# Attention scores of both heads in one full-height product, from batch 3 on

## The chip, the cores and the metric

The kernel runs on one core of a Trainium2 chip. Its time is the device time of one launch in microseconds (us), the median of three runs. One further run was made under the hardware profiler; "the profile" and "the trace" are of that run. TensorE is called PE in it, VectorE DVE, ScalarE ACT, GpSimd POOL and SyncE SP. Line numbers (L266 and so on) are those of the kernel before.

## What is computed

Eight batches of eight heads, 576 positions, head dimension 64. Each head has causal attention with a sparse mask: the first four heads of a batch see the last 32 positions, the last four see the positions of the same remainder modulo 32. The 4608 rows of 512 values that come out go through a two-layer projection with a leaky activation in between.

```python
scores = scale * np.matmul(q, k.transpose(0, 1, 3, 2))
mask_local = (rel >= 0) & (rel < stride)                       # stride = 32
mask_strided = (rel >= 0) & (pos[None, :] % stride == pos[:, None] % stride)
...                                                            # local for h < 4, strided for h >= 4
attn = np.exp(scores - max); attn = attn / (sum + 1e-09)
x = (attn @ v).transpose(0, 2, 1, 3).reshape(B * S, H * D)
h = x @ w_in                                                   # 512 -> 2048
g = np.maximum(h, 0.0) + alpha * np.minimum(h, 0.0)
out = g @ w_out                                                # 2048 -> 512
```

## The kernel before

All products are in 16-bit floats with 32-bit sums. A **unit** is half a batch, four local or four strided heads; a unit has two **pairs** of heads, numbered g from 0 to 31. The two heads of a pair lie one above the other in the partitions: head 0 in rows 0 to 63, head 1 in rows 64 to 127.

The attention is cut into small pieces, each a Python function that issues its instructions for all engines:

- `transpose_piece(u, "q")` and `(u, "k")`: eight PE transposes (L209) of a unit's queries or keys into a PSUM tile tp, and copies from there to SBUF: from batch 2 on one copy on DVE for queries (to qT, L156) and one on ACT for keys (to kT, L154). Each covers 128 rows and 1024 elements. After the keys, `tails` does the last 64 positions of both: two or four more transposes (L232, L237) and small copies, queries on DVE and keys on ACT.
- `score_piece(P, i)`: a pair has two. For every block of queries (96 of a local pair, 72 of a strided one) and for each head there is a product (L266) of the head's 64 rows of kT with its 64 rows of qT. Head 0 writes one PSUM bank of the tile sp, head 1 another. A local piece has three blocks, six products; a strided one four blocks, eight products. ACT takes the exponential of both banks at once into an SBUF tile et (L290), and from batch 2 on POOL multiplies it with a mask of zeros and ones (L300).
- `pv_piece(P, a)`: et is the stationary operand, the values with a column of ones the moving one (L313). DVE takes reciprocals of the sums (L320) and scales (L322).
- `x_piece(P)`: PE transposes (L330) and a copy to xT (L334 on ACT for strided pairs, L338 on DVE for local ones).

The projections are cut into pieces too. `lin1_piece(n, m)` makes 128 hidden features of 512 rows: four products of 512 columns (L483), or eight where the rows wrap round in xT; then ACT makes `neg` (L493), and the DVE instruction L496, which makes gT and frees the PSUM tile hps, is put on a list `late` and issued after the next attention piece. `lin2_piece(n, i)` makes four products (L528) of the 16 that add into one PSUM tile ops; after the sixteenth ACT copies it out (L533).

The order on every engine is the program's, and it is written out by hand: the function `tile_strided_..._kernel` alternates projection pieces with attention pieces (`attn_step`). Batches 0 and 1 run partly by themselves at the start. Batch 2 lies among the second-layer pieces of row block 0 and the first half of block 1; batch 3 lies where two pieces of the first layer come on each one of the second; batches 4 to 7 lie among alternating lin2 and lin1 pieces of row blocks 2 to 5. The last projections have no attention left beside them.

PSUM buffers: three of the tag "ps" (tp, the tails' tt, pv and xp take turns), two of "hps", one "ops" and one "sp" of two banks. POOL's queue also issues most loads and casts queries and keys to 16 bits; SP's queue issues later local loads and the stores.

Of the kernel before, what the change touches and what calls it, by code (L numbers as in the profile page):

```python
# [9 lines left out]
F32 = mybir.dt.float32  # L10
F16 = mybir.dt.float16
ALU = mybir.AluOpType
AF = mybir.ActivationFunctionType
# [18 lines left out]
def kernel(  # L32
# [10 lines left out]
    nc = tc.nc  # L43
    keep = tc.keep_in_program_order

    B, H, S, D = q.shape
    NT = B * S
    NCH = NT // 512
    SCALE = 1.0 / float(np.sqrt(D))
# [4 lines left out]
    cpool = ctx.enter_context(tc.tile_pool(name="const", bufs=1))  # L54
# [10 lines left out]
    pbpool = ctx.enter_context(tc.tile_pool(name="pb", bufs=1, space=bass.MemoryType.PSUM))  # L65
# [5 lines left out]
            name=nc.get_next_instruction_name(), act_func_set_id=6, ins=[], outs=[]  # L71
# [4 lines left out]
    alpha_r = cpool.tile([16, 128], F32)  # L76
    oma = cpool.tile([128, 16], F32)
    madd = cpool.tile([128, 360], F16)
    ident = consts[:, 0:128]
    mfirst, mother, mstr = consts[:, 128:416], consts[:, 224:320], consts[0:72, 416:488]  # L80

# [3 lines left out]

    NE = 6
    qTs = [cpool.tile([128, 2, S], F16, name=f"qT{i}") for i in range(2)]
    kTs = [cpool.tile([128, 2, 672], F16, name=f"kT{i}") for i in range(2)]
    vls = [cpool.tile([128, 24, 65], F16, name=f"vl{i}") for i in range(2)]
    vss = [cpool.tile([128, 4, 8, 65], F16, name=f"vs{i}") for i in range(2)]  # L90
    ets = [cpool.tile([128, 640], F16, name=f"et{i}") for i in range(NE)]


    loaded = {}
# [57 lines left out]
    def cast_copy(eng, o, i):  # L152
        if eng == "act":
            keep(nc.scalar.copy(o, i))  # L154
        elif eng == "dve":
            keep(nc.vector.tensor_copy(o, i))  # L156
        else:
            keep(nc.gpsimd.tensor_copy(o, i))
# [18 lines left out]
    ectr = {"i": 0}  # L177
    wide = {"on": True}
    NEARLY = 2

    def make_pair(g):
        P = Pair()
        P.g, P.b, P.hp = g, g // 4, g % 4
        P.strided = P.hp >= 2
        P.pr = P.hp % 2
        P.n, P.w = (8, 72) if P.strided else (6, 96)
        u = g // 2
        P.qT, P.kT = qTs[u % 2][:, g % 2], kTs[u % 2][:, g % 2]
        P.sgroups = ([0, 1, 2, 3], [4, 5, 6, 7]) if P.strided else ([0, 1, 2], [3, 4, 5])
        P.pgroups = ([0, 1, 2], [3, 4, 5], [6, 7]) if P.strided else P.sgroups  # L190
        P.et = {}
        P.x16 = None
        return P

    def transpose_piece(u, nm):

        b, strided = u // 2, u % 2 == 1
        early = b < NEARLY
        src = cast16[(b, strided, nm)]
        dst = qTs[u % 2] if nm == "q" else kTs[u % 2][:, :, 32:608]
        tp = pspool.tile([128, 8, 64, 2], F16, tag="ps", name="tp")
        for j in range(8):
            blk = (src[:, j % 2, 128 * (j // 2) : 128 * (j // 2) + 128] if strided
                   else src[:, j].rearrange("p f d -> p (f d)"))
            keep(nc.tensor.transpose(tp[:, j].rearrange("r p e -> r (p e)"), blk, ident))  # L209
        if strided:  # L210
            main = tp.rearrange("r j p e -> r e j p")
            o = dst.rearrange("r e (j p) -> r e j p", j=8)[:, :, :, 0:64]
        else:
            main = tp.rearrange("r t p e -> r e p t")
            o = dst[:, :, 0:512].rearrange("r e (p t) -> r e p t", t=8)
        if early:
            for e in range(2):
                eng = "dve" if (nm == "q") == (e == 0) else "act"
                if nm == "k" and e == 1:
                    tails(b, u, strided)  # L220
                cast_copy(eng, o[:, e : e + 1], main[:, e : e + 1])
            return
        cast_copy("dve" if nm == "q" else "act", o, main)
        if nm == "k":
            tails(b, u, strided)

    def tails(b, u, strided):
        tl = cast16[(b, strided, "tail")]
        tt = pspool.tile([128, 1024], F16, tag="ps", name="tt")
        if strided:  # L230
            for h in range(4):
                keep(nc.tensor.transpose(  # L232
                    tt[:, 64 * h : 64 * h + 64], tl[0:64, 128 * h : 128 * h + 128],
                    ident[0:64, 0:64]))
        else:
            for e in range(2):
                keep(nc.tensor.transpose(  # L237
                    tt[:, 128 * e : 128 * e + 128], tl[:, 128 * e : 128 * e + 128], ident))
        for i, (o, eng) in enumerate(((qTs[u % 2], "dve"), (kTs[u % 2][:, :, 32:608], "act"))):
            if strided:  # L240
                tv = tt[:, 0:256].rearrange("r (e f i p t) -> r i e t f p", e=2, f=2, i=2, p=8)
                ov = o.rearrange("r e (t f p) -> r e t f p", t=4, f=2)
                for e in range(2):
                    cast_copy(eng, ov[:, e, :, :, 64:72], tv[:, i, e])
            else:
                tv = tt[:, 0:256].rearrange("r (e i p) -> r i e p", e=2, i=2)
                cast_copy(eng, o[:, :, 512:576], tv[:, i])

    def score_piece(P, i):

        et = ets[ectr["i"] % NE]
        if wide["on"] and ectr["i"] % 2:
            sps = [phpool.tile([128, 512], F32, tag="hps", name="sph") for _ in range(2)]
        else:
            sp = pbpool.tile([128, 2, 512], F32, tag="sp", name="sp")
            sps = [sp[:, y] for y in range(2)]
        ectr["i"] += 1
        w, grp = P.w, P.sgroups[i]
        n = w * len(grp)
        r = 72 if P.strided else 128  # L260
        early = P.b < NEARLY
        for x, t in enumerate(grp):
            k0 = 32 + 72 * t if P.strided else 96 * t
            for y in range(2):
                hf = slice(64 * y, 64 * y + 64)
                keep(nc.tensor.matmul(  # L266
                    sps[y][:, w * x : w * x + w], P.kT[hf, k0 : k0 + 128],
                    P.qT[hf, w * t : w * t + w], start=(x == 0),
                    stop=(x == len(grp) - 1 and not early), skip_group_check=True))

                key = (2 * (t // 2) + y, t % 2) if P.strided else (t, y)
                P.et[key] = (et, n * y + w * x)
        first = not P.strided and i == 0
        if early:

            if first:
                m = madd[:, 0:288]
            else:
                m = madd[0:72, 288:360] if P.strided else madd[:, 96:192]
                m = m.unsqueeze(1).to_broadcast([r, n // w, w])  # L280
            for y in range(2):
                keep(nc.tensor.matmul(
                    sps[y][:, 0:n], ident[0:r, :], m, start=False, stop=True, skip_group_check=True))
        ev = et[0:r, 0 : 2 * n]
        if wide["on"] and ectr["i"] % 2 == 0:
            for y in range(2):
                keep(nc.scalar.activation(
                    ev[:, n * y : n * y + n], sps[y][0:r, 0:n], AF.Exp, scale=SCALE))
        else:
            keep(nc.scalar.activation(  # L290
                ev.rearrange("r (y c) -> r y c", y=2), sp[0:r, :, 0:n], AF.Exp, scale=SCALE))
        if early:
            return
        if first:
            ev = ev.rearrange("r (y c) -> r y c", y=2)
            m = mfirst.unsqueeze(1).to_broadcast([r, 2, n])
        else:
            ev = ev.rearrange("r (c f) -> r c f", f=w)
            m = (mstr if P.strided else mother).unsqueeze(1).to_broadcast([r, 2 * n // w, w])
        keep(nc.gpsimd.tensor_tensor(ev, ev, m, op=ALU.mult))  # L300
# [38 lines left out]

    npair = 4 * B  # L340
    pairs = [make_pair(g) for g in range(npair)]
    pieces = []

# [3 lines left out]
    def T(u, nm):  # L347
        return lambda: transpose_piece(u, nm)

    def Sc(g, i):  # L350
        return lambda: score_piece(pairs[g], i)
# [40 lines left out]
    for g in range(7, npair + 2):  # L392
        a, p, t, x = g, g - 1, g + 1, g - 2
# [23 lines left out]
        todo = [(g // 4, pr) for pr in range(2)] if g % 4 == 0 and 8 <= g < npair else []  # L417

        if g % 4 == 1 and 9 <= g and g // 4 + 1 < B:
            todo = [(g // 4 + 1, nm) for nm in "qk"]  # L420
# [149 lines left out]
        keep(nc.vector.memset(kTs[i][:, :, 0:32], 0.0))  # L570
        keep(nc.vector.memset(kTs[i][:, :, 608:672], 0.0))
    for t in ets:
        keep(nc.vector.memset(t[:, 576:640], 0.0))
    keep(nc.gpsimd.memset(vls[0][0:32, 0:1, 0:64], 0.0))
    keep(nc.gpsimd.memset(vls[0][:, :, 64:65], 1.0))
    keep(nc.gpsimd.memset(vss[0][:, :, :, 64:65], 1.0))
# [37 lines left out]
            attn_step(0)  # L614

    wide["on"] = False

    for c in range(4):
        load_w(c, True)
# [83 lines left out]
```

## Time and profile before

| | |
|---|---|
| median of 3 runs | 354.89 us (353.97 to 355.74) |
| the profiled execution | 355.82 us |
| its span, first to last instruction | 354.1 us |
| mean granted TensorE clock | 0.978 |
| score products on PE (L266) | 448, from 12.6 to 261.9 us |
| query copies of 128x1024 on DVE (L156) | 12, mean 1216 ns |
| gT on DVE (L496) | 144, mean 743 ns |
| exponentials of two banks on ACT (L290) | 58, about 650 ns |
| masks on POOL (L300) | 48, mean 1281 ns |

A matmul's duration in the trace reaches from its start to the end of its own result, so neighbours overlap; the pace of PE is read from the starts. A line of the timeline merges neighbours of one kind: its duration reaches to the end of the last.

### The profile page before, as it was taken

To read this page: it belongs to the slowest core of one execution; us is meant where nothing else is said; L and a number is where in the kernel's file an instruction comes from. 1 tells how busy PE (TensorE), PEld (TensorE's weight loads), DVE (VectorE), ACT (ScalarE), POOL (GpSimd) and SP (SyncE) were. 2 spreads that over 40 slices of the span, in tenths; PEclk is the share of its full clock that TensorE was granted. 3 is DMA by queue.
4 is the path that set the end of the run, shared out by engine and by line. 5 is a ranking of instruction groups with operands and counts; after the bars stand their busy time and mean duration, and the time that the engine had idled before them with its cause. 6 is when DMAs were issued, how large, how long until landed. Compare 5 with 4: busy or idle time off the path is not lost.

```text
span 354.1 us, 6755 instructions
## 1 busy us (share of the span) xinstructions
PE 337.4 (95%) x2733; PEld 176.7 (50%) x2733; DVE 196.9 (56%) x389; ACT 178.6 (50%) x315; POOL 145.6 (41%) x163
## 2 busy tenths in 40 slices
PE   6999979999898998999999999999999999999995
PEld 2454545445444554454566674545455444444443
DVE  2367784785444777566656665666565444444400
ACT  2554863674344574556565655565555444444411
POOL 7935425439985674557355532451240000000000
PEclk9899995999999999999999999999999999999999
DMA  8999999933945772562656120000000100100021
GB/s 174 203 204 229 209 268 133 200 44 63 145 88 182 85 171 33 98 63 44 177 98 65 39 57 31 31 31 31 30 31 30 62 30 30 62 30 30 31 89 59
DMA packets 46010, 32.84 MB, mean 93 GB/s; under 512 B 27276, under 2 KB 37884, under 8 KB 45980
## 3 DMA queue, kind: packets, MB, share of 16 engines
q0 software_dynamic: 37456, 17.01, 44.8%
q1 hardware_dynamic: 8524, 15.41, 12.3%
q8 instruction: 21, 0.34, 0.4%
q14 instruction: 9, 0.07, 0.1%
HBM read 36.83 MB, written 9.44 MB: 131 GB/s over the span
## 4 chain that ended last, share of the span: by engine, by line
PE 85%; DVE 4%; POOL 4%; ACT 4%; DMA 2%; issue 1%; ACTq 0%; POOLq 0%
PE hps L483 35%; PE ops L528 32%; PE tp L209 4%; PE pv L313 3%; PE sp L266 3%; PE xp L330 2%; DMA qs<-in_q_dram 2%; DVE x L322 2%; PE wps L550 2%; POOL et L300 2%; PE ops L519 1%; DVE gT L496 1%; ACT kT L154 1%; ACT neg L493 1%; ACT osb L533 1%
## 5 line engine op out<-in xcount | busy, mean ns | idle before, releaser
L496 DVE SCALAR_TENSOR_TENSOR gT<-neg,oma,hps 128x512 f16<-128x512 f32 x144 | 106.9, 743 | 75.2 <-ACT neg L493 72.8
L483 PE MATMUL hps<-xT,win 128*128 128x512 f16 (+1 forms) x640 | 146.1, 360 | 0.1
L528 PE MATMUL ops<-wout,gT 128*128 128x512 f16 x560 | 141.9, 379 | 1.9 <-ACT osb L533 1.4
L493 ACT ACTIVATE neg<-hps 128x512 f32<-128x512 f32 x144 | 86.2, 599 | 94.2 <-PE hps L483 93.2
L300 POOL TENSOR_TENSOR et<-et,consts 128x576 f16<-128x576 f16 (+1 forms) x48 | 61.4, 1281 | 80.4 <-ACT et L290 80.2
L483 PEld LDWEIGHTS <-win 128*128 128x128 f16 x640 | 58.3, 98 | 52.5 <-issue 2.6
L528 PEld LDWEIGHTS <-gT 128*128 128x128 f16 x560 | 49.7, 98 | 50.7 <-issue 2.5
L290 ACT ACTIVATE et<-sp 72x576 f16<-72x576 f32 (+1 forms) x58 | 37.6, 649 | 21.1 <-PE sp L266 13.7
L322 DVE TENSOR_TENSOR x<-pv,rc 72x384 f16<-72x384 f32 (+2 forms) x80 | 42.1, 527 | 2.7
L320 DVE RECIPROCAL rc<-pv 72x6 f32<-72x6 f32 (+2 forms) x80 | 14.9, 186 | 42.9 <-PE pv L313 42.5
L533 ACT COPY osb<-ops 128x512 f32<-128x512 f32 x35 | 20.5, 587 | 27.9 <-PE ops L528 27.9
L313 PEld LDWEIGHTS <-et 72*128 72x128 f16 (+1 forms) x448 | 23.4, 99 | 17.9 <-issue 4.2
L266 PEld LDWEIGHTS <-kT 64*128 64x128 f16 x448 | 11.1, 96 | 25.8 <-issue 18.3
L156 DVE COPY qT<-tp 128x1024 f16<-128x1024 f16 (+1 forms) x16 | 17.4, 1084 | 6.8 <-PE tp L209 6.8
L154 ACT COPY kT<-tp 128x1024 f16<-128x1024 f16 (+1 forms) x16 | 14.5, 908 | 10.4 <-PE tp L209 10.4
L266 PE MATMUL sp<-qT,kT 64*128 64x72 f16 (+1 forms) x408 | 17.7, 202 | 1.6 <-ACT kT L154 1.0
L313 PE MATMUL pv<-vs,et 72*128 72x65 f16 x256 | 15.7, 193 | 2.5 <-ACT qT L154 1.3
L550 PE MATMUL wps<-wrm 128*128 128x512 f16 x44 | 16.3, 445 | 1.2 <-DVE wrm L562 1.2
L330 PEld LDWEIGHTS <-x 72*128 72x128 f16 (+1 forms) x224 | 12.6, 102 | 7.8 <-DVE x L322 2.4
L330 PE MATMUL xp<-consts,x 72*128 72x72 f16 (+1 forms) x224 | 14.9, 208 | 1.0 <-DVE x L322 0.8
L334 ACT COPY xT<-xp 128x576 f16<-128x576 f16 x16 | 10.2, 640 | 6.0 <-PE xp L330 5.9
L313 PE MATMUL pv<-vl,et 128*128 128x65 f16 x192 | 12.0, 200 | 1.3 <-DVE vl L156 1.1
(66 smaller groups left out, 195.4 us busy)
## 6 DMA issues: line engine op xcount, KB each, us to landing
out_dram<-osb SPq DMA_DIRECT2D x35, 256.0 KB, 2.0
ql<-in_q_dram SPq DMA_DIRECT2D x5, 512.0 KB, 4.8
kl<-in_k_dram SPq DMA_DIRECT2D x5, 512.0 KB, 6.9
vl<-in_v_dram POOLq DMA_DIRECT2D x8, 288.0 KB, 7.4
qs<-in_q_dram POOLq DMA_DIRECT2D x8, 256.0 KB, 5.5
ks<-in_k_dram POOLq DMA_DIRECT2D x8, 256.0 KB, 6.4
win<-in_moe_w_in_dram POOLq DMA_DIRECT2D x4, 512.0 KB, 11.5
wout<-in_moe_w_out_dram POOLq DMA_DIRECT2D x4, 512.0 KB, 17.9
```

What stands on the lines that cost most here:

```text
L266: keep(nc.tensor.matmul(sps[y][:, w * x : w * x + w], P.kT[hf, k0 : k0 + 128], P.qT[hf, w * t : w * t + w], start=(x == 0), stop=(x == len ...
L290: keep(nc.scalar.activation(ev.rearrange("r (y c) -> r y c", y=2), sp[0:r, :, 0:n], AF.Exp, scale=SCALE))
L300: keep(nc.gpsimd.tensor_tensor(ev, ev, m, op=ALU.mult))
L313: keep(nc.tensor.matmul(pv[:, 65 * x : 65 * x + 65], et[0:r, c : c + 128], v16[0:r, 2 * P.pr + hh, t, :] if P.strided else v16[:, 6 * (2 * ...
L322: keep(nc.vector.tensor_tensor(P.x16[0:w, c0 : c0 + 64 * nb].rearrange("r (c e) -> r c e", e=64), pvv[:, :, 0:64], rc[0:w, 0:nb].unsqueeze ...
L330: keep(nc.tensor.transpose(xp[:, P.w * t : P.w * t + P.w], P.x16[0 : P.w, 128 * t : 128 * t + 128], ident[0 : P.w, 0 : P.w]))
L483: keep(nc.tensor.matmul(hps[:, dst : dst + w], win16[:, kk, 128 * m : 128 * m + 128], xT[:, kk, src : src + w], start=(kk == 0 and x == 0) ...
L493: keep(nc.scalar.activation(neg, hps, AF.Relu, scale=-1.0))
L496: keep(nc.vector.scalar_tensor_tensor(gTs[n][:, m, :], neg, oma[:, m : m + 1], hps, op0=ALU.mult, op1=ALU.add))
L528: keep(nc.tensor.matmul(ops, gTs[n][:, kf, 128 * mt : 128 * mt + 128], wout16[:, kf, :], start=(kf == 0), stop=(kf == 15)))
L533: keep(nc.scalar.copy(osb, ops))
L550: keep(nc.tensor.matmul(wps, wrm[:, 0:128], wrm, start=True, stop=True))
```

## The change

From batch 3 on (`NPAD = 3`) queries are kept in a second layout, qpad: for each pair two copies of the width of S, both 128 rows high. The first holds head 0 in rows 0 to 63 and zeros below, the second zeros above and head 1 in rows 64 to 127. A product of all 128 rows of kT with both halves of qpad then gives the scores of both heads beside each other. `score_full` makes one such product for every block of queries: 144 columns for a strided block, 192 for a local one, two blocks in a PSUM bank. A strided piece has four blocks as before; a local pair is now cut into four blocks and two, in place of three and three. The exponential takes the two banks (or one) at once. The mask of the four local blocks is written out in full (`mloc`); the others are broadcast as before.

The query copy of a unit becomes two on DVE, rows 0 to 63 and rows 64 to 127, and the query part of `tails` likewise; the key part is issued first. The tiles et grow from 640 to 832 columns. The zeros of qpad and the mask `mloc` are written by POOL, in four memsets and two copies that stand after batch 0 and ahead of the loads of w_out.

```diff
+    mloc = cpool.tile([128, 8, 96], F16)
+    qpads = [cpool.tile([128, 2, 2, S], F16, name=f"qpad{i}") for i in range(2)]
-    ets = [cpool.tile([128, 640], F16, name=f"et{i}") for i in range(NE)]
+    ets = [cpool.tile([128, 832], F16, name=f"et{i}") for i in range(NE)]
...
-        cast_copy("dve" if nm == "q" else "act", o, main)
+        if nm == "q" and b >= NPAD:
+            for y in range(2):
+                hf = slice(64 * y, 64 * y + 64)
+                o = qpads[u % 2][hf, :, y, :]
+                o = (o.rearrange("r e (j p) -> r e j p", j=8)[:, :, :, 0:64] if strided
+                     else o[:, :, 0:512].rearrange("r e (p t) -> r e p t", t=8))
+                cast_copy("dve", o, main[hf])
+        else:
+            cast_copy("dve" if nm == "q" else "act", o, main)
...
-        for i, (o, eng) in enumerate(((qTs[u % 2], "dve"), (kTs[u % 2][:, :, 32:608], "act"))):
+        full, half = slice(0, 128), [slice(0, 64), slice(64, 128)]
+        todo = [(1, full, kTs[u % 2][:, :, 32:608], "act")]
+        if b >= NPAD:
+            todo += [(0, half[y], qpads[u % 2][half[y], :, y, :], "dve") for y in range(2)]
+        else:
+            todo += [(0, full, qTs[u % 2], "dve")]
+        for i, hf, o, eng in todo:
...
+    def score_full(P, i):
+        et = ets[ectr["i"] % NE]
+        sp = pbpool.tile([128, 2, 512], F32, tag="sp", name="sp")
+        ectr["i"] += 1
+        w = P.w
+        grp = P.sgroups[i] if P.strided else ([0, 1, 2, 3], [4, 5])[i]
+        for x, t in enumerate(grp):
+            k0 = 32 + 72 * t if P.strided else 96 * t
+            c0 = 2 * w * (x % 2)
+            keep(nc.tensor.matmul(
+                sp[:, x // 2, c0 : c0 + 2 * w], P.kT[:, k0 : k0 + 128],
+                P.qpad[:, :, w * t : w * t + w], start=(x % 2 == 0), stop=(x % 2 == 1),
+                skip_group_check=True))
+            for y in range(2):
+                key = (2 * (t // 2) + y, t % 2) if P.strided else (t, y)
+                P.et[key] = (et, 2 * w * x + w * y)
+        r = 72 if P.strided else 128
+        nb, n = len(grp) // 2, 4 * w
+        ev = et[0:r, 0 : nb * n]
+        keep(nc.scalar.activation(
+            ev.rearrange("r (y c) -> r y c", y=nb), sp[0:r, 0:nb, 0:n], AF.Exp, scale=SCALE))
+        if not P.strided and i == 0:
+            m = mloc.rearrange("r c f -> r (c f)")
+            keep(nc.gpsimd.tensor_tensor(ev, ev, m, op=ALU.mult))
+            return
+        ev = ev.rearrange("r (c f) -> r c f", f=w)
+        m = (mstr if P.strided else mother).unsqueeze(1).to_broadcast([r, ev.shape[1], w])
+        keep(nc.gpsimd.tensor_tensor(ev, ev, m, op=ALU.mult))
+
     def score_piece(P, i):
+        if P.b >= NPAD:
+            score_full(P, i)
+            return
...
-        keep(nc.vector.memset(t[:, 576:640], 0.0))
+        keep(nc.vector.memset(t[:, 576:832], 0.0))
...
     wide["on"] = False
+    for t in qpads:
+        keep(nc.gpsimd.memset(t[64:128, :, 0, :], 0.0))
+        keep(nc.gpsimd.memset(t[0:64, :, 1, :], 0.0))
+    for c0, c1, m in ((0, 2, mfirst[:, 0:96]), (2, 8, mother)):
+        keep(nc.gpsimd.tensor_copy(
+            mloc[:, c0:c1, :], m.unsqueeze(1).to_broadcast([128, c1 - c0, 96])))
```

More of the change, by code (lines that the diff above doesn't have):

```diff
@@ L179 @@
     NEARLY = 2
+    NPAD = 3
     def make_pair(g):
@@ L187, in make_pair @@
         u = g // 2
-        P.qT, P.kT = qTs[u % 2][:, g % 2], kTs[u % 2][:, g % 2]
+        P.qT, P.kT, P.qpad = qTs[u % 2][:, g % 2], kTs[u % 2][:, g % 2], qpads[u % 2][:, g % 2]
         P.sgroups = ([0, 1, 2, 3], [4, 5, 6, 7]) if P.strided else ([0, 1, 2], [3, 4, 5])
@@ L238, in tails @@
                     tt[:, 128 * e : 128 * e + 128], tl[:, 128 * e : 128 * e + 128], ident))
-        for i, (o, eng) in enumerate(((qTs[u % 2], "dve"), (kTs[u % 2][:, :, 32:608], "act"))):
+        full, half = slice(0, 128), [slice(0, 64), slice(64, 128)]
[5 more added lines that the diff above has]
+        for i, hf, o, eng in todo:
             if strided:
-                tv = tt[:, 0:256].rearrange("r (e f i p t) -> r i e t f p", e=2, f=2, i=2, p=8)
+                tv = tt[hf, 0:256].rearrange("r (e f i p t) -> r i e t f p", e=2, f=2, i=2, p=8)
                 ov = o.rearrange("r e (t f p) -> r e t f p", t=4, f=2)
@@ L245, in tails @@
             else:
-                tv = tt[:, 0:256].rearrange("r (e i p) -> r i e p", e=2, i=2)
+                tv = tt[hf, 0:256].rearrange("r (e i p) -> r i e p", e=2, i=2)
                 cast_copy(eng, o[:, :, 512:576], tv[:, i])
+    def score_full(P, i):
[26 more added lines that the diff above has]
+        keep(nc.gpsimd.tensor_tensor(ev, ev, m, op=ALU.mult))
     def score_piece(P, i):
+        if P.b >= NPAD:
+            score_full(P, i)
+            return
         et = ets[ectr["i"] % NE]
```

## The prediction

> **What bounds the kernel now.** I read the page first: busy shares, then the chain that ended last.
>
> ```profile
> PE 337.4 (95%) x2733; PEld 176.7 (50%) x2733; DVE 196.9 (56%) x389; ACT 178.6 (50%) x315; POOL 145.6 (41%) x163
> ...
> PE 85%; DVE 4%; POOL 4%; ACT 4%; DMA 2%; issue 1%; ACTq 0%; POOLq 0%
> ```
>
> TensorE (PE) bounds it, and whatever shortens PE's stream between 97 us (first score piece of batch 3) and 262 us (last one) shortens the run: what follows is projection matmuls without a pause. In the list of waits, the weight load of the score line has an entry that no engine explains:
>
> ```profile
> PEld L266 <- issue: 18.3, 46, 0.5
> ```
>
> The timeline of PE tells what it is. Columns: start, duration, engine, line, operation, tiles, shape, count.
>
> ```profile
> 184.17 1.03 PE L528 MATMUL ops<-wout,gT 128*128 128x512 f16 x4
> 185.13 0.30 PE L266 MATMUL sp<-qT,kT 64*128 64x72 f16 x8
> 185.36 1.05 PE L483 MATMUL hps<-xT,win 128*128 128x256 f16 x8
> 186.25 0.35 PE L313 MATMUL pv<-vl,et 128*128 128x65 f16 x6
> 186.43 1.02 PE L528 MATMUL ops<-wout,gT 128*128 128x512 f16 x4
> ```
>
> Starts give the true pace (durations overlap). Elsewhere in that view 512-column products follow each other every 0.216 us (0.864 for four) and 256-column ones every 0.109. So L528 is through at 184.17+0.864=185.034, yet the scores start at 185.13: 0.095 lost. The eight scores start over 0.108 us, the last streams 0.03, and L483 could start at 185.27; it starts at 185.36: 0.095 lost again. The 128-row neighbours lose nothing: L483 to L313 is 185.36+8x0.109=186.23, and six L313 take 0.18. A score piece thus occupies PE for 0.33 us, of which 0.19 is idle.
>
> [...] Score products use 64 rows, their neighbours 72 to 128[...]. [...] fewer rows save no time; the trace agrees (L322 384-element pieces take 553 ns on 72 rows and on 96). [...] the vl copy, which reads from row 96, starts at 133.72, after its predecessor's end (132.95+0.73), where usual successors start 0.07 to 0.09 before it.
>
> **The change part by part.**
>
> PE. Strided pieces become four 144-column products, a local pair six of 192 (four, then two). [...] 4x62.5=0.250 us, and 6x82.5=0.495 for a pair, 0.2475 a piece[...]. Their moving operand has two runs (head 0, head 1); the nearest row is L282, whose 288 columns in four runs of 72 have 40.46 to 40.72 for two, 130 ns against 122.5. I take nothing for it, and keep 4 ns a product as the upper end. Weight loads stay hidden: 128-row loads keep up with L313 at 0.03 us a product. A piece saves 0.33-0.25=0.082 us.
>
> There are 40 pieces in batches 3 to 7, not all worth that:
> - Six wait for the key copy on ACT (starts 97.42, 114.54, 146.27, 181.74, 217.33, 252.80; L483 is through at 181.55 and the scores start at 181.74). [...] the start stays; from first score to next product it took 0.235 and will take 0.250: -0.08 in all.
> - Two end in another wait: after 99.93 PE waits for the ops eviction (L533, until 100.45), after 132.80 for the vl copy on DVE (until 134.31). Nothing won.
> - Two lie in the window of the first stall below. That leaves 30 x 0.082 = 2.46 us.
>
> DVE. The query copy, one instruction over 128 rows, becomes two of 64 rows and the same 1024 elements:
>
> ```profile
> L156 DVE COPY qT<-tp 128x1024 f16<-128x1024 f16 x12 | 14.6, 1216 | 2.3 <-PE tp L209 2.3
> L322 DVE TENSOR_TENSOR x<-pv,rc 72x384 f16<-72x384 f32 x32 | 17.7, 553 | 1.1
> L322 DVE TENSOR_TENSOR x<-pv,rc 96x384 f16<-96x384 f32 x32 | 17.7, 553 | 1.1
> ```
>
> Each half costs what the whole did, and as the second half starts at row 64 both it and its successor are held: what follows comes 2x1.23 us after the start instead of 1.14, so 1.33 later. This occurs in ten transpose steps. DVE has idle time overall, so I went through what is queued behind each copy. Where PE runs only the second projection (steps at 91.57, 106.30) nothing urgent follows. In the steady steps (154.06, 189.56, 225.12 local; 170.04, 205.59, 241.10 strided) the gT instruction behind it frees an hps buffer that PE wants two L483 groups later; at 205.59 it now ends near 206.29+2.46+0.75=209.5, and PE asks at 209.78: covered with 0.2 to spare. Two steps aren't covered.
>
> First, strided batch 4, PE and then DVE:
>
> ```profile
> 134.46 1.03 PE L483 MATMUL hps<-xT,win 128*128 128x512 f16 x4
> 135.32 0.61 PE L209 MATMUL tp<-consts,qs 128*128 128x128 f16 x8
> 135.77 1.03 PE L483 MATMUL hps<-xT,win 128*128 128x512 f16 x4
> ...
> 136.89 1.03 PE L528 MATMUL ops<-wout,gT 128*128 128x512 f16 x4
> 137.90 1.89 PE L483 MATMUL hps<-xT,win 128*128 128x512 f16 x8
> ```
> ```profile
> 135.97 1.23 DVE L156 COPY qT<-tp 128x1024 f16<-128x1024 f16 x1 [0.53 <-PE tp L209]
> 137.11 1.40 DVE L496 SCALAR_TENSOR_TENSOR gT<-neg,oma,hps 128x512 f16<-128x512 f32 x2
> ```
>
> Here a projection piece stands ahead of the transpose, so its gT instruction queues behind the copy. L528 was through at 137.75, and L483 started at 137.90, as the first gT ended (137.11+0.74): PE is already waiting on DVE. With gT 1.33 later it starts at 139.24: -1.34 us. The ops eviction wait after it (141.33) hangs on PE itself and gives nothing back.
>
> Second, local batch 4:
>
> ```profile
> 124.24 0.35 PE L313 MATMUL pv<-vs,et 72*128 72x65 f16 x6
> ...
> 125.84 0.29 PE L313 MATMUL pv<-vs,et 72*128 72x65 f16 x4
> ...
> 127.04 0.30 PE L266 MATMUL sp<-qT,kT 64*128 64x96 f16 x6
> ```
> ```profile
> 122.16 1.21 DVE L156 COPY qT<-tp 128x1024 f16<-128x1024 f16 x1
> ...
> 124.85 0.55 DVE L322 TENSOR_TENSOR x<-pv,rc 72x384 f16<-72x384 f32 x1
> ```
>
> The pv of 125.84 takes the buffer (three of them) that this L322 frees, at 125.40 now. Query halves until 124.62, xT copy 0.37, gT 0.70, reciprocal 0.23, L322 0.55: 126.47. PE, 0.08 earlier than before, arrives at 125.76 and waits until 126.52. Its projection (0.13 and 0.87 later) brings the score piece to 127.52 and the next product to 127.77, against 127.28: -0.49, both pieces' gains included.
>
> Tails. Twice as many small query copies, 0.16 to 0.36 us more per unit on DVE; the key tail, now written ahead of them, is on ACT, so neither queue changes its order. A score piece now waits for the later half copy and, once, for POOL's memsets; behind it on PE everything would queue, but the halves are done over 1.5 us ahead of every first score. The strided scores at 146.27 wait for ACT's key tail (146.17); the third small query copy ends near 145.9: covered, and without that cover up to 0.2 us in five places.
>
> ACT and POOL. Exponentials of 768 and 384 columns replace two of 576: at 645 ns for 576 and the same fixed part the sum is equal. Masks likewise (1286 ns for 576): the first local one ends some 0.6 us later with the exponential, needed over 3 us later. Nothing.
>
> Start-up. Four POOL memsets of 1152 elements and two copies (192 and 576) go ahead of the w_out loads and all later entries of POOL's queue. POOL's own copies run 1024 elements in 1.04 us; so at most 5.6 us[...]. Behind them wait the casts of 34.89 and 36.33, whose transposes are at 46.39 and 49.29, and w_out (first used at 76.39): hidden, as POOL also idles 3.7 us there for transfers. SP's queue isn't touched. Six wider memsets of et on DVE, 85 ns for 64 columns, so at most 1.5 us more, come while DVE waits 3.9 us for its first values. Nothing.
>
> Sum: 2.46-0.08-1.34-0.49 = 0.55 us won. The profiled execution took 355.82 (span 354.1 and 1.7 around), so 355.27; the median shown is 354.89, 0.93 lower, so **354.3**.
>
> **Rivals.**
> - Gain undamped (0.15): the held copies overlap or buffers come free otherwise, so neither stall appears. For it: DVE idles 44% of the span. Against: both chains are in the trace end to end. 32 x 0.082-0.08: 2.5 us won, 352.3.
> - Slower, DVE the bound (0.15): half-height copies take longer than 1.23 us; the trace has none that starts at row 64. Place: gT and L322 behind them. At 1.55 us the two stalls grow by 0.64 each and the three strided steps exceed their 0.2 by 0.44: 2.6 us, 356.9. It decides from about 1.5 us on.
> - The change doesn't remove the 0.19 (0.05): if this is the price of a waiting score piece[...], 30 x 0.19 = 5.7 us come back: 360.0. Against: L313 waits for semaphores too and loses nothing, and the 64-row tail transposes (L232) lose 0.095 at both ends.
> - Start-up not hidden (0.05): POOL's 5.6 us meet casts with 9 us of slack; 0 to 1 us, 354.3 to 355.3.
>
> **How the numbers follow.** The forecast has 0.60, its own range 353.3 to 355.9: 140 products x 4 ns and up to 0.9 us from the three strided steps above, half the stalls below. The range, 352.2 to 356.5, takes in the undamped gain and leaves out the two slower rivals, 2 in 10. A measurement can tell about 0.5%, 1.77 us, from no change. Faster by more: the undamped rival and an edge, 0.16; slower: 0.18; within: 0.66.
>
> **What would show it.** Right: score products starting 62 and 82 ns apart, L528 to scores without the 0.095; query copies of 64 rows at 1.2 us, 1.33 us more ahead of gT; PE waiting on gT 1.5 us near 138. Wrong: gaps around 128-row scores; PE waits on gT in each strided transpose step; PE waits in the first 80 us that weren't there.

## The result and the profile after

The changed kernel takes 359.44 us (median of 4 runs, 358.94 to 361.43), against 354.56 for the kernel before, run with it: 1.44% slower, with an interval of 0.97% to 1.91%. The forecast was 354.3 with a range of 352.2 to 356.5. Here and below, ratios and intervals leave out launches in a slower state (over 1.5% above the fastest of the same kernel) and medians count all, so a ratio need not be the quotient of the two medians. The profiled execution has a span of 357.5 us, where before had 354.1.

The page of the changed kernel: busy shares, the chain that ended last, and the group of the query copies.

```profile
PE 335.0 (94%) x2593; PEld 182.5 (51%) x2593; DVE 211.8 (59%) x414; ACT 177.8 (50%) x315; POOL 150.1 (42%) x169
...
PE 79%; DVE 8%; ACT 5%; POOL 4%; issue 2%; DMA 2%; ACTq 0%; POOLq 0%
...
L158 DVE COPY qpad<-tp 64x1024 f16<-64x1024 f16 x20 | 24.4, 1219 | 1.9 <-PE tp L212 1.7
```

PE's share of the chain fell from 85% to 79%, and DVE's and ACT's rose. A half-height query copy takes 1219 ns, the whole one took 1216. The list of waits of the changed kernel names what PE now stands for (us in total, times, longest):

```profile
DVE qpad L158 <- ACT kT L156: 9.8, 9, 1.5
...
PE sp L276 <- DVE qpad L158: 5.2, 5, 1.8
...
PE hps L533 <- DVE gT L546: 1.3, 1, 1.3
```

Five waits of score pieces for queries, 5.2 us, are new. So is the first line, which I had not expected at all: DVE's copies of the query tails wait for ACT's *key* copies. The score pieces themselves are as forecast. PE of the changed kernel, the place shown before at 184 to 186 us:

```profile
187.97 1.03 PE L578 MATMUL ops<-wout,gT 128*128 128x512 f16 x4
188.84 0.41 PE L276 MATMUL sp<-qpad,kT 128*128 128x144 f16 x4
189.09 1.04 PE L533 MATMUL hps<-xT,win 128*128 128x256 f16 x8
189.96 0.35 PE L363 MATMUL pv<-vl,et 128*128 128x65 f16 x6
```

Scores start 0.87 us after the four L578 did, with no gap, and hold PE for 0.25 us in place of 0.33. Both gaps of 0.095 us are gone: in this trace the first score product starts within 0.001 us of the moment when the product ahead is through, wherever it waits for nothing, and so does the product behind the last.

**Where the time came from.** The 1232 starts of projection products in the two traces can be matched by number. The difference between them, after minus before, moves in steps, and each step has a place. From 97.65 us of the kernel before to the last projection it grows from 0.52 to 3.91, by 3.39 us:

| place (time in the trace before) | us |
|---|---|
| first strided scores of batches 3 to 7 (114.78, 146.51, 181.98, 217.57, 253.03) | 5 x +0.84 |
| strided batch 4, projection of 137.90 | +1.36 |
| local batch 4, up to 125.97 | +0.75 |
| two small ones (97.65, 134.46) | +0.28 |
| the rest, mostly 0.083 for a strided piece and 0.166 for a local pair | -3.2 |

In the first 97 us all the traces differ from each other; these are taken up below.

### The profile page after: what moved, and what is told of

Read it like the earlier page. It is cut to its first block, busy times and chain, and to the rows that moved or that the text cites. A ratio compares the mean times of both kernels' runs of the same rounds, so it can differ in the third digit from the quotient of the medians.

```text
span 357.5 us, 6512 instructions
## 1 busy us (share of the span) xinstructions
PE 335.0 (94%) x2593; PEld 182.5 (51%) x2593; DVE 211.8 (59%) x414; ACT 177.8 (50%) x315; POOL 150.1 (42%) x169
## 4 chain that ended last, share of the span: by engine, by line
PE 79%; DVE 8%; ACT 5%; POOL 4%; issue 2%; DMA 2%; ACTq 0%; POOLq 0%
PE hps L533 32%; PE ops L578 30%; PE tp L212 3%; PE pv L363 3%; PE sp L276 3%; DVE qpad L158 2%; PE xp L380 2%; DVE x L372 2%; DMA qs<-in_q_dram 2%; ACT kT L156 2%; DVE gT L546 2%; POOL et L350 2%; PE wps L600 1%; ACT neg L543 1%; PE ops L569 1%
## 5 line engine op out<-in xcount | busy, mean ns | idle before, releaser
L578 PE MATMUL ops<-wout,gT 128*128 128x512 f16 x560 | 141.8, 379 | 1.9 <-ACT osb L583 1.6
L533 PEld LDWEIGHTS <-win 128*128 128x128 f16 x640 | 59.9, 98 | 52.5 <-issue 4.8
L578 PEld LDWEIGHTS <-gT 128*128 128x128 f16 x560 | 50.3, 98 | 50.1 <-issue 2.7
L294 POOL TENSOR_TENSOR et<-et,consts 72x576 f16<-72x576 f16 (+1 forms) x30 | 34.6, 1155 | 66.6 <-ACT et L286 66.5
L286 ACT ACTIVATE et<-sp 72x576 f16<-72x576 f32 (+2 forms) x40 | 25.9, 648 | 19.1 <-PE sp L276 16.1
L158 DVE COPY qpad<-tp 64x1024 f16<-64x1024 f16 x20 | 24.4, 1219 | 1.9 <-PE tp L212 1.7
L290 POOL TENSOR_TENSOR et<-et,mloc 128x768 f16<-128x768 f16 x10 | 16.5, 1649 | 16.6 <-ACT et L286 16.6
L276 PE MATMUL sp<-qpad,kT 128*128 128x144 f16 (+1 forms) x140 | 16.5, 234 | 5.2 <-DVE qpad L158 5.2
L276 PEld LDWEIGHTS <-kT 128*128 128x128 f16 x140 | 11.4, 97 | 14.5 <-ACT neg L543 5.1
L340 ACT ACTIVATE et<-sp 72x576 f16<-72x576 f32 (+1 forms) x18 | 11.7, 648 | 8.9 <-PE sp L332 6.4
```

Source lines behind the costliest of these rows:

```text
L276: keep(nc.tensor.matmul(sp[:, x // 2, c0 : c0 + 2 * w], P.kT[:, k0 : k0 + 128], P.qpad[:, :, w * t : w * t + w], start=(x % 2 == 0), stop= ...
L286: keep(nc.scalar.activation(ev.rearrange("r (y c) -> r y c", y=nb), sp[0:r, 0:nb, 0:n], AF.Exp, scale=SCALE))
L533: keep(nc.tensor.matmul(hps[:, dst : dst + w], win16[:, kk, 128 * m : 128 * m + 128], xT[:, kk, src : src + w], start=(kk == 0 and x == 0) ...
L578: keep(nc.tensor.matmul(ops, gTs[n][:, kf, 128 * mt : 128 * mt + 128], wout16[:, kf, :], start=(kf == 0), stop=(kf == 15)))
```

## The experiments

Each run was timed beside runs of the kernel before on the same chip. "Shift" is the difference of projection starts against the trace of the kernel before, from 97 us on, unless said otherwise.

**The order of the tails.** In `tails` the change issues the key part first, where the kernel before had the query part first. This is so in all batches, not only from batch 3 on, where the change was said to lie.

```diff
-        todo = [(1, full, kTs[u % 2][:, :, 32:608], "act")]
         if b >= NPAD:
-            todo += [... query halves ...]
+            todo = [... query halves ...]
         else:
-            todo += [(0, full, qTs[u % 2], "dve")]
+            todo = [(0, full, qTs[u % 2], "dve")]
+        todo += [(1, full, kTs[u % 2][:, :, 32:608], "act")]
```

> The changed kernel with only the order of the two tail parts put back: the query tail is issued ahead of the key tail, in all batches. Theory (order): the query tail copies on DVE and the key tail copies on ACT read one PSUM tile and are made to follow each other in program order; with keys first the query tail waits for ACT's big key copy and tail, and the first strided scores wait for it, 0.84 us in each of five batches and 0.37 in batches 1 and 2, 4.9 us in all. Expected 354.5 us, with no wait of the scores on DVE left over 0.1 us. Rival (DVE load): the scores wait because DVE has twice the query copies, whatever their order; the waits stay and the time stays at 358.5 to 359.5.

Measured: 354.01 us against 355.22, ratio 0.9965 (0.9940 to 0.9990). The five steps of 0.84 are 0.15 now, and no score piece waits for DVE. The same step in three kernels shows why; first the kernel before, ACT, DVE and PE:

```profile
145.09 1.01 ACT L154 COPY kT<-tp 128x1024 f16<-128x1024 f16 x1 [0.90 <-PE tp L209]
146.00 0.34 ACT L154 COPY kT<-tt 128x64 f16<-128x64 f16 x2
```
```profile
145.31 0.35 DVE L156 COPY qT<-tt 128x64 f16<-128x64 f16 x2
```
```profile
146.27 0.30 PE L266 MATMUL sp<-qT,kT 64*128 64x72 f16 x8
```

Then the changed one, in the same order:

```profile
147.88 1.01 ACT L156 COPY kT<-tp 128x1024 f16<-128x1024 f16 x1 [0.90 <-PE tp L212]
148.79 0.34 ACT L156 COPY kT<-tt 128x64 f16<-128x64 f16 x2
```
```profile
149.16 0.73 DVE L158 COPY qpad<-tt 64x64 f16<-64x64 f16 x4 [1.15 <-ACT kT L156]
```
```profile
148.00 1.04 PE L533 MATMUL hps<-xT,win 128*128 128x512 f16 x4
149.89 0.41 PE L276 MATMUL sp<-qpad,kT 128*128 128x144 f16 x4 [0.86 <-DVE qpad L158]
```

DVE is idle for 1.15 us, until 0.03 us after ACT's key tail ends at 149.13, and only then copies the query tail. PE is through at 148.86 and waits for these copies. The one that holds it longest is the third of the four, the second half of the first pair (149.52 to 149.75):

```profile
149.52 0.23 DVE L158 COPY qpad<-tt 64x64 f16<-64x64 f16 x1
```

The fourth ends at 149.89, as the scores start, which is too late to have released them: in the run below and in the next one the scores start 0.05 us after the end of the copy that releases them. With the query tail first (DVE, ACT, PE):

```profile
145.46 0.73 DVE L158 COPY qpad<-tt 64x64 f16<-64x64 f16 x4
```
```profile
145.24 1.01 ACT L156 COPY kT<-tp 128x1024 f16<-128x1024 f16 x1 [0.90 <-PE tp L212]
146.28 0.33 ACT L156 COPY kT<-tt 128x64 f16<-128x64 f16 x2
```
```profile
146.55 0.42 PE L276 MATMUL sp<-qpad,kT 128*128 128x144 f16 x4 [0.15 <-ACT kT L156]
```

DVE does its part while ACT is still at the big key copy. ACT's tail then starts at 146.28, after DVE's four copies (until 146.19), where in the kernel before it started 0.10 ahead of the big copy's end; that is most of the 0.15 left.

**The order alone, in the old kernel.** Nothing of the change but this order:

```diff
-        for i, (o, eng) in enumerate(((qTs[u % 2], "dve"), (kTs[u % 2][:, :, 32:608], "act"))):
+        for i, o, eng in ((1, kTs[u % 2][:, :, 32:608], "act"), (0, qTs[u % 2], "dve")):
```

> The kernel before with only that order swapped: key tail ahead of query tail, no other part of the change. Theory (order): the strided scores now wait for two query tail copies (0.36 us) that start after ACT's key tail; they start some 0.4 to 0.5 us later in each of batches 3 to 7 and 0.37 in batches 1 and 2, so 2.8 to 3.2 us slower than before: 357.5. Rival (DVE load): without the doubled copies the order makes no difference, 354.6.

Measured: 358.38 against 355.22, ratio 1.0076 (1.0056 to 1.0096), which is 2.7 us. From 97 us on the shift has five steps and no other, 0.37 each; batches 0 to 2 add about 0.4 in this trace. DVE and PE of this run at one of the five:

```profile
147.47 0.35 DVE L156 COPY qT<-tt 128x64 f16<-128x64 f16 x2 [1.15 <-ACT kT L154]
```
```profile
146.30 1.04 PE L483 MATMUL hps<-xT,win 128*128 128x512 f16 x4
147.74 0.31 PE L266 MATMUL sp<-qT,kT 64*128 64x72 f16 x8 [0.40 <-DVE qT L156]
```

The order costs by itself. Here the scores start 0.05 us after the first of two small copies ends. In the changed kernel they need the third of four, which ends 0.37 us after the first, and start 0.15 us after it: that makes 0.37 into 0.84.

**Why DVE waits for ACT.** Both tails are read from one PSUM tile, tt. This run keeps the changed order, and transposes the tails twice into two tiles, one for each reader.

```diff
+        tts = {}
+        for i in (1, 0):
+            tts[i] = tt = pspool.tile([128, 1024], F16, tag="ps", name=f"tt{i}")
             ... the transposes, into tt ...
...
         for i, hf, o, eng in todo:
+            tt = tts[i]
```

> The changed kernel, key tail still issued first, but the tail transposes are made twice into two PSUM tiles, one that ACT reads for the keys and one that DVE reads for the queries; this costs PE 0.12 us in each of 16 units. Theory: the query tail waits for ACT only because both read one tile; the strided scores' waits on DVE (five, 5.2 us) shrink below 0.2 us each, and the time is some 2.3 us less than the changed kernel's, 357. Rival: DVE waits for ACT or comes late for another reason; the waits stay at 0.8 us and more and the time rises by the transposes' 1.9 us to 361.

Measured: 357.50 against 355.53, ratio 1.0080 (1.0048 to 1.0112). No score piece waits for DVE. DVE and PE at the same step:

```profile
149.38 0.73 DVE L158 COPY qpad<-tt 64x64 f16<-64x64 f16 x4 [0.21 <-PE tt L245]
```
```profile
148.93 0.40 PE L245 MATMUL tt<-consts,tl 64*128 64x64 f16 x8
149.27 1.04 PE L536 MATMUL hps<-xT,win 128*128 128x512 f16 x4
150.22 0.42 PE L279 MATMUL sp<-qpad,kT 128*128 128x144 f16 x4
```

With a tile of its own DVE waits for the transposes alone, runs beside ACT, and the scores start 0.09 us after the projection is through. From 97 us on to the last projection the shift, 2.16 us, comes out unchanged, where the changed kernel's grew by 3.39. So the wait comes from the shared tile. The run as a whole is still slower than the kernel before; one cost ahead of 97 us is that the second set of tail transposes, at 77.13 us, waits 0.86 us for ACT's key copy. Both engines only read the tile: in the changed kernel DVE's first read starts 0.03 us after ACT's last one ends (149.16 and 149.13), here it starts 0.57 us ahead of ACT's key tail (149.38 and 149.95). The runs don't show whether the tile or its PSUM bank counts, as this run gave each reader both, nor what makes the second reader wait. The kernel before had shown such a wait of one reader for the other, in a line of its waits that I passed over (batches 0 and 1 copy the halves of one tp on both engines):

```profile
ACT qT L154 <- DVE qT L156: 3.2, 4, 1.4
```

**The second half copy, alone.** The old kernel with one more DVE copy of rows 64 to 127, into a tile that nobody reads.

```diff
         cast_copy("dve" if nm == "q" else "act", o, main)
+        if nm == "q" and b >= 3:
+            o = spare[64:128]
+            ...
+            cast_copy("dve", o, main[64:128])
```

> The kernel before, and from batch 3 on a second query copy on DVE of rows 64 to 127 into a tile that nobody reads; nothing else. Theory: the doubled copy alone makes the two stalls of local and strided batch 4: 1.36 us more at the projection of 137.90 and 0.8 to 1.0 us more around 126 to 134, and nothing in the other eight transpose steps; 2.2 to 2.4 us slower than before, 357.5. Rival: the stalls need the new score piece (its longer exponentials and masks); then under 0.5 us, 355.4.

Measured: 357.40 against 355.53, ratio 1.0069 (1.0037 to 1.0101). The shift has +0.67 at 125.97, of which 0.11 is given back, and +1.37 at 137.90: 1.9 us in all, in the two steps foretold, and nothing in the other eight. That is less than the 2.2 to 2.4 expected: the first of them came out at 0.56 in place of 0.8 to 1.0. The changed kernel at these two, PE and then DVE, first strided batch 4:

```profile
138.51 1.03 PE L578 MATMUL ops<-wout,gT 128*128 128x512 f16 x4
140.88 1.46 PE L533 MATMUL hps<-xT,win 128*128 128x512 f16 x6 [1.34 <-DVE gT L546]
```
```profile
137.59 2.46 DVE L158 COPY qpad<-tp 64x1024 f16<-64x1024 f16 x2 [0.53 <-PE tp L212]
140.07 1.41 DVE L546 SCALAR_TENSOR_TENSOR gT<-neg,oma,hps 128x512 f16<-128x512 f32 x2
```

The two copies take 2.46 us, and gT starts 2.48 after the start of the first; before it was 1.14. Then local batch 4:

```profile
125.22 0.35 PE L363 MATMUL pv<-vs,et 72*128 72x65 f16 x6
...
127.57 0.29 PE L363 MATMUL pv<-vs,et 72*128 72x65 f16 x4 [0.58 <-DVE x L372]
```
```profile
123.23 2.45 DVE L158 COPY qpad<-tp 64x1024 f16<-64x1024 f16 x2
...
126.96 0.55 DVE L372 TENSOR_TENSOR x<-pv,rc 72x384 f16<-72x384 f32 x1
```

**A cure for the first of them that failed.** gT is issued ahead of the query copies where one is pending (on top of the query tail first).

```diff
         if nm == "q" and b >= NPAD:
+            while late:
+                late.pop(0)()
             for y in range(2):
```

> As the run with the query tail first, and besides a gT instruction that is pending at a query transpose piece from batch 3 on is issued ahead of the query copies on DVE, not behind them. Theory: the wait of the first projection on gT near 138 us (1.34 us in the changed kernel's trace) is this queueing and goes entirely; 1.4 us less than with the query tail first alone, 353.1. Rival: the projection waits for another holder of its buffer; no difference, 354.5.

Measured: 355.15 against 355.22, ratio 0.9986 (0.9956 to 1.0015), and against the run with the query tail first a shift of -1.50 at that projection and +1.48 at the next. PE and DVE:

```profile
138.60 1.03 PE L535 MATMUL hps<-xT,win 128*128 128x512 f16 x4
140.94 1.02 PE L535 MATMUL hps<-xT,win 128*128 128x512 f16 x4 [1.31 <-DVE gT L548]
```
```profile
136.99 0.75 DVE L548 SCALAR_TENSOR_TENSOR gT<-neg,oma,hps 128x512 f16<-128x512 f32 x1 [0.71 <-ACT neg L545]
137.66 2.45 DVE L158 COPY qpad<-tp 64x1024 f16<-64x1024 f16 x2
140.14 1.41 DVE L548 SCALAR_TENSOR_TENSOR gT<-neg,oma,hps 128x512 f16<-128x512 f32 x2
```

My expectation was wrong. One gT moved ahead, but the next projection's gT still stands behind the copies, and PE waits for that one. The stall belongs to DVE's 2.46 us, not to the place of one instruction.

**The scores without the second half copy.** Query tail first, and only the first half of each query copy, of the tails' too. The second half of qpad is filled with zeros, so head 1's queries are left out and the result is not the whole one.

```diff
-            for y in range(2):
+            for y in range(1):
```

> The changed kernel with the query tail first and only the first half of each query copy (main and tail) made from batch 3 on, so head 1's queries are left out there (its scores are those of zero queries); every other instruction stays. Theory: the score products win their 0.083 us a piece in 33 or so pieces and both DVE stalls are gone: 2.7 to 2.9 us less than before, 352.4. Rival: the score pieces lose elsewhere what they win (exponentials of 768 columns, masks of 768); no better than the run with both copies and the query tail first, 355.

Measured: 352.37 against 355.53, ratio 0.9901 (0.9862 to 0.9939). The shift falls by 2.65 us: this is what the score products win when neither DVE nor the tails take it back.

**The zeros later.** The memsets and mask copies of POOL, moved from ahead of the w_out loads to behind batch 3's first loads.

```diff
     wide["on"] = False
-    for t in qpads:
-        ... four memsets, two copies ...
     for c in range(4):
         load_w(c, True)
...
     load_unit(3, True, False)
+    for t in qpads:
+        ... four memsets, two copies ...
     end2 = attn_until(2)
```

> As the run with the query tail first, and besides the four memsets and two mask copies of POOL are issued later, ahead of batch 2's pieces and behind the loads of batch 3, where POOL has no work for some 10 us. Theory: their 5.4 us ahead of the second layer's weights are hidden already; no difference from the run with the query tail first, within 0.4 us. Rival: they delay the start; 0.5 to 1.5 us less.

Measured: 355.36 against 355.22, ratio 0.9992 (0.9964 to 1.0019). Against the run with the query tail first the starts lie 1.41 us apart at 26.7 us, before the first memset is issued, and 1.47 at the end. The start-up hides them.

**The order in the first batches.** The old kernel, key tail first in batches 0 to 2 alone.

```diff
-        for i, (o, eng) in enumerate(((qTs[u % 2], "dve"), (kTs[u % 2][:, :, 32:608], "act"))):
+        todo = [(0, qTs[u % 2], "dve"), (1, kTs[u % 2][:, :, 32:608], "act")]
+        for i, o, eng in (todo[::-1] if b < 3 else todo):
```

> The kernel before, with the key tail issued first in batches 0 to 2 alone (the order that the change also gives to these). Theory: the strided steps of batches 1 and 2 lose 0.37 us each, and batch 2's is given back a few pieces later where a pv piece waits for POOL's mask anyway; 0.4 us slower than before, about 355.8. Rival: the stall in batch 1 also leaves TensorE longer at the lower clock around 60 us, in every launch; 1.3 us or more slower, 356.8. That would also explain why the times of the changed kernel lie further from before's than the two traces do.

Measured: 356.55 against 355.69, ratio 1.0041 (1.0019 to 1.0062). By the ratio that is 1.5 us, between the medians 0.86, and between the medians of the six launches of each at a mean granted clock of 0.980 it is 0.80. The trace has the two steps of 0.37 and the return of 0.35, so 0.4 us are explained. The interval leaves 0.3 to 1.8 us more, and that part stays open. The clock around 60 us could hold it: between 59 and 66 us it was granted at 0.63 in this trace, 0.76 in before's and 0.67 in the changed kernel's. But a run with the query tail first had 0.64 there too, and another 0.88, so one trace each doesn't settle it.

**A version that keeps the gain.** Query tail first, and DVE makes one full-height query copy as before; POOL copies its halves into qpad.

```diff
+        cast_copy("dve" if nm == "q" else "act", o, main)
         if nm == "q" and b >= NPAD:
             for y in range(2):
-                ...
-                cast_copy("dve", o, main[hf])
+                ... o: rows hf of qpad, i: the same rows of qT ...
+                cast_copy("pool", o, i)
```

> The changed kernel with the query tail first; from batch 3 on DVE makes the one full-height query copy as before, and POOL copies its halves from there to the zero-padded tile; the tails stay on DVE in halves. Theory: both DVE stalls go, the tails' 0.15 us in five strided steps stays, POOL has the room: 2.1 us less than before, 353.1, faster than both kernels. Rival: POOL's copies, 1 us each, delay its masks, and the pv pieces wait for these: 355 or more.

Measured: 352.99 against 355.53, ratio 0.9933 (0.9905 to 0.9961); the shift falls by 1.95 us. DVE, POOL and PE at strided batch 4:

```profile
131.34 1.23 DVE L158 COPY qT<-tp 128x1024 f16<-128x1024 f16 x1 [0.60 <-PE tp L212]
132.48 1.40 DVE L547 SCALAR_TENSOR_TENSOR gT<-neg,oma,hps 128x512 f16<-128x512 f32 x2
```
```profile
132.63 2.13 POOL L160 COPY qpad<-qT 64x1024 f16<-64x1024 f16 x2 [0.59 <-DVE qT L158]
```
```profile
133.28 1.89 PE L534 MATMUL hps<-xT,win 128*128 128x512 f16 x8
```

gT follows the copy by 1.14 again, PE has no long wait, and POOL's 2.13 us fall where its queue has room.

**The tails by pair.** On top of that, the strided tails are issued query and key of the first pair, then of the second.

```diff
-        for i, hf, o, eng in todo:
-            if strided:
-                ...
-                for e in range(2):
+        if strided:
+            for e in range(2):
+                for i, hf, o, eng in todo:
                     ...
                     cast_copy(eng, ov[:, e, :, :, 64:72], tv[:, i, e])
```

> The run whose queries POOL spreads, and besides the strided tails issued pair by pair: query and key parts of the first pair, then of the second. Theory: ACT's key tail of the first pair then follows two small query copies, not four, and the first strided scores wait only for that pair; the 0.15 us in five steps go: 0.7 us less than the run whose queries POOL spreads, 352.3. Rival: ACT's big key copy ends later than the query tails anyway, no difference, 353.

Measured: 352.32 against 355.69, ratio 0.9898 (0.9859 to 0.9937). The five steps of 0.15 shrink by 0.12 each. By its median this is the fastest version that computes the whole result, 1.0% faster than before.

**From batch 2 on.** On top of that again:

```diff
-    NPAD = 3
+    NPAD = 2
```

> As the run with the tails by pair, with the new scores from batch 2 on. Theory: up to six more pieces win 0.083 us, 0.5 us less, 351.8. Rival: in batch 2 POOL's queue has no room (a pv piece already waits 0.84 us for a mask there), and four copies of 1 us more delay masks: 0.5 to 2 us more, 353 to 354.

Measured: 355.34 against 355.69, ratio 1.0000 (0.9969 to 1.0031): the rival, and more of it than it said, 3.0 us over the run with the tails by pair. PE and POOL of that run in batch 2:

```profile
84.85 0.41 PE L279 MATMUL sp<-qpad,kT 128*128 128x144 f16 x4 [2.45 <-POOL qpad L160]
85.28 1.69 PE L581 MATMUL ops<-wout,gT 128*128 128x512 f16 x4
```
```profile
80.09 1.65 POOL L293 TENSOR_TENSOR et<-et,mloc 128x768 f16<-128x768 f16 x1
81.68 1.04 POOL L160 CAST ql<-ql 128x1024 f16<-128x1024 f32 x1
82.67 2.13 POOL L160 COPY qpad<-qT 64x1024 f16<-64x1024 f16 x2
```

Here the copies stand behind a mask and a cast of the next batch, and the scores wait for them, where the rival had named the pv pieces and the masks. The wait is not all of the loss: from 85.5 to 88.9 us the 512-column products behind it start 0.42 to 0.43 us apart in place of 0.216. The clock granted between 84 and 92 us was 0.79 in this trace and 1.00 in before's.

## Why the prediction was wrong

- **The step that failed** is the one on the tails: "the key tail, now written ahead of them, is on ACT, so neither queue changes its order". The queues don't, but the two engines read one PSUM tile, and the one that was issued second waited, 1.15 us at the step shown. I looked at DVE's queue and ACT's queue and not at the tile between them. I put the third small copy at 145.9 against a key tail at 146.17, "covered", and 0.2 us in five places as the most; the sum has no term for it. It took 0.69 in each of the five (0.84 with keys first, 0.15 with queries first). That is 3.4 of the 3.9 us that lie, from 97 us on, between the 0.55 forecast as a gain and the 3.39 lost.
- I also read the order as part of "from batch 3 on". It holds for all batches, and costs 0.7 to 2.2 us in batches 0 to 2 by the interval of that run. The traces place 0.4 of it; the cause of the rest is open. With the 3.39 us from 97 us on, the placed part is 3.8 us. The medians of the four launches of each kernel differ by 4.88, with an interval of 3.4 to 6.8 us, so they can't check the rest.
- **PE's gain** was right: the two gaps of 0.095 gone, products at 62 and 83 ns, no price for the two runs of the moving operand: the line through the 109 ns of 256 columns and the 216 ns of 512 has 62 at 144 columns and 82 at 192. The forecast had 0.082 for every piece; it is 0.083 for a strided one, and for a local pair nothing in the first piece (four products of 83 ns against 0.331 us) and 0.166 in the second. The run without the second half copy won 2.65 us; the sum had 2.46 for 30 pieces, and the rival with the gain undamped 2.5 for 32.
- **The stall of strided batch 4** was forecast at 1.34 and was 1.36 in the changed kernel and 1.37 in the old one with a bare second copy. That of local batch 4 was forecast at 0.49 with both pieces' gains; with the query tail first it was 0.59. The held second half was right too: gT came 1.34 us later (2.48 less 1.14), where the forecast had 1.33 (its own 2x1.23 less 1.14 makes 1.32). In all ten steps the second half, which starts at row 64, begins 0.013 or 0.014 us after the first has ended, and in the nine where the instruction behind it was ready that one begins 0.031 or 0.032 us after the second has ended; behind a full-height copy a ready one began 0.078 to 0.085 us ahead of the end. Among the four small copies of the strided tails the third, the first of rows 64 to 127, begins 0.013 or 0.014 us after its predecessor's end, the second and fourth, on the rows of their predecessors, 0.074 to 0.080 us ahead of it.
- **The three strided steps with 0.2 to spare** held. So did the start-up; POOL's memsets and copies took 5.2 us there, where 5.6 were allowed.
- **The 0.15 us per strided unit** that four small copies cost ACT's key tail was missed: 0.74 us, the same shared tile seen from the other side. With it the forecast kernel is the one with the query tail first: from 97 us on its starts lose 0.06 us against before's, in place of winning 0.55.
- **The rivals.** "The change doesn't remove the 0.19" came nearest to the time (360.0), by luck: the 0.19 is gone. "DVE the bound" (356.9) had the direction, but not by its mechanism: the half copies took 1.22 us, not 1.55. "Gain undamped" (352.3) is about what the two repaired versions reach (352.99 and 352.32).

## What to carry to other kernels

When an edit reorders instructions on different engines, look at what they share: in these runs two engines that read one PSUM tile went one after the other in program order (DVE idle for 1.15 us, until 0.03 us after ACT's last read), so the reader that is ready first should be issued first. A zero-padded full-height product was worth its wasted rows here, where short 64-row products stood among full-height ones: of 0.33 us a piece, 0.19 went on the two changes between 128 and 64 rows. Then ask who writes the padded operand: here two half-height copies cost as much as two full ones (2.46 us, where a full one took 1.216), and belonged on the engine that had room, at that stage, not on average.

## What the runs showed of the hardware

- A change between 64-row products and 72- or 128-row ones cost PE 0.089 to 0.099 us each way in the kernel before (a score's own stream taken as 32 and 42 ns, the pace of L330 with 72 and 96 columns), at every score piece from 97 us on that waited for nothing else and at the 64-row transposes of the tails; among 72-, 96- and 128-row products such a change cost 0.003 us at most where nothing else was waited for.
- Launches of one kernel differ by several us (351.2 to 357.7 for the kernel before). This goes with the mean granted clock: its launches at 0.997 took 351.2 to 351.8 us, those at 0.976 took 357.2 to 357.7. The traces differ in the first 64 us: the first projection starts anywhere from 26.4 to 28.2 us, and the clock between 59 and 66 us was 0.61 to 1.00. From 97 us on two traces of kernels that differ in one place agree to about 0.02 us elsewhere (in the five pairs of the order alone, the second half copy, the early gT, the later zeros and the tails by pair). So a step of 0.1 us can be read from matched starts where medians can't tell it.
- POOL copied 64 rows by 1024 16-bit values within SBUF in 1.04 us, in less time than DVE took from PSUM (1.22).
